# Sums of the seven half-size products moved from GpSimd to VectorE, and the tokens added by accumulating DMAs

## The chip, the cores and the metric

One core of one Trainium2 chip. The time is the device time of one execution in microseconds (us), the median of three runs; a profiled execution of the same program gives the trace. Engines are called TensorE (PE), VectorE (DVE), ScalarE (ACT), GpSimd (POOL) and SyncE (SP, which only issues DMAs here).

## The reference

An attention with mixing between heads, and behind it a token mixer and a channel mixer, all float32. The change lies in the channel mixer alone:

```python
u = x + h.transpose(0, 2, 1)                   # x, u: batch 4, 448 tokens, 768 features
h2 = np.maximum(u @ w_ch1, 0.0) @ w_ch2        # w_ch1: 768 x 1536, w_ch2: 1536 x 768
return (u + h2).astype(np.float32)
```

## The kernel before

Features lie on the partitions, tokens along the free axis. The 4 x 448 = 1792 tokens of `u` are in a DRAM tensor `u_dr` of 128 x 6 x 1792 (six tiles of 128 features).

**Split operands.** Every operand of the mixers is split into a high half (a cast to fp32r on ScalarE) and a low half (the float32 value less the high half, a subtraction on VectorE or GpSimd). One product is then three matmuls, lines 653 to 655: high x high, high x low of the second operand, low x high. The names are `wh`, `wl` for the first operand (weights), `uh`, `ul` or `rh`, `rl` for the second (tokens).

**First half of the channel mixer** (lines 889 to 921): tokens 0 to 511 (g = 0), then 512 to 767 (g = 1), in 12 chunks c of 128 hidden features. `ch1` computes a chunk (18 matmuls into `pc`), `relu_split` makes `rh` on ScalarE and `rl` on VectorE (line 650), and `ch2` of the chunk before (18 more) adds it into six PSUM banks `po`. The order on an engine is the order in which the code calls it. Between the products stand `cv_tick` (it converts the 64-bit weights of the input to float32 tiles `wt`: two instructions on VectorE at lines 456 and 460 and a third at 466, a clamp on GpSimd at 438, an absolute value on ScalarE at 432) and `split(eng)`, which splits the weights of a coming chunk, `wh` on ScalarE (412), `wl` on `eng` (413). Split number 2c belongs to `ch1` of chunk c, 2c + 1 to `ch2`.

**The stages** (lines 926 to 933): the last 1024 tokens, from SB0 = 768, go through both layers by a scheme of seven half-size products instead of eight (2 x 2 blocks, `ORDER`). For the first layer there are two groups g of seven products, for the second seven products in two halves h: 28 stages of 27 matmuls of 128 x 128 by 128 x 512. `us` holds the tokens, `rr` the hidden values. For stage n + 2 `prep_s` computes sums of quarters in place (`sum_`, line 809, on GpSimd; `w` 128 x 1152 for products 5, 6, 3 and 7, `x` 128 x 1536 for 5, 6, 7 and 4), then the high halves (835, ScalarE) and the low halves (836, VectorE), in slot n % 3 of `wslot` and `xslot`. So three stages' operands exist at a time, and those of n + 2 may be written as soon as stage n - 1 has been multiplied. `mm_s(n)` multiplies into three banks, `psx` or `psz`; the two sets are used in turn and accumulate over several products. `evict(n)` reads them out: copies on ScalarE (882, 884) or additions on VectorE (886; 877 in the second layer), `relus` on ScalarE (864). In the second layer `us` itself is the accumulator: it still holds the tokens, each product is added to it, and `store_out` writes a finished quarter to the output through SP's queue (756). As the sums of the first layer destroy one quarter of the tokens in `us`, it is loaded again from `u_dr` at stage 13 (line 933).

Of the kernel before, what the change touches and what calls it, by code (L numbers as in the profile page):

```python
# [14 lines left out]
ALU = mybir.AluOpType  # L15
# [24 lines left out]
def attn_mixer_kernel(  # L40
# [12 lines left out]
    nc = tc.nc  # L53
# [6 lines left out]
    u_dr = dram.tile([128, KD, B * S], F32, name="u_dr")  # L60
# [224 lines left out]
    p = pair("w", "pw")  # L285
# [116 lines left out]
    SP, split_at = {}, [0]  # L402

    def split(eng):
        n = split_at[0]
        split_at[0] += 1
        c, w = divmod(n % (2 * NC), 2)
        while cv_pos[0] <= min(4 * c + 2 * w + 5, len(units) - 1):
            cv_tick(1)
        src = WT[w, c // 3][:, c % 3, :]  # L410
        hi, lo = [y[:, :768] for y in wslot(n % 6)]
        nc.scalar.copy(out=hi, in_=src)
        eng.tensor_tensor(out=lo, in0=src, in1=f32(hi), op=ALU.subtract)  # L413
# [57 lines left out]
    def cv_tick(k, eng=nc.gpsimd):  # L471
        for _ in range(k):
            i = cv_pos[0]
            if i >= cv_lim[0]:
                return
            if i + 5 < len(units):
                cv_load(i + 5)
            cv_step(i, eng)
            if 0 <= i + 2 < len(units):
                cv_clamp(i + 2)  # L480
            if 0 <= i + 3 < len(units):
                cv_abs(i + 3)
            cv_pos[0] += 1
# [19 lines left out]
    for T in range(2, NT):  # L503
        hi = (sf[T] - 8) // 2
# [276 lines left out]
    def ch2(g, c, ds=range(KD)):  # L781
        i0, n = CB[g]
        ws = SP[2 * NC * g + 2 * c + 1]
        for d in ds:
            if c == 0:
                OP[g, d] = psb.tile([128, 512], F32, tag=f"o{d}", name=f"po{d}")
            mm3(OP[g, d][:, :n], [w[:, 128 * d:128 * d + 128] for w in ws], RL[g, c], c == 0, c == NC - 1)
            if c == NC - 1:
                o = UR[g][:, d, :n]
                nc.vector.tensor_tensor(out=o, in0=OP.pop((g, d))[:, :n], in1=o, op=ALU.add)  # L790
                o_row[0] = d
                store_out(i0, o)
# [12 lines left out]
        t, d = (us, 3 * j) if L == 0 else (rr, 6 * j + 3 * s)  # L805
        return t[:, d:d + 3, HN * k:HN * k + HN]

    def sum_(out, in0, in1, op=ALU.subtract):
        nc.gpsimd.tensor_tensor(out=out, in0=in0, in1=in1, op=op)  # L809

    def prep_s(n):
        L, g, p, h = stages[n]
        whi, wlo = [y.rearrange("p (a n) -> p a n", a=3) for y in wslot(n % 3)]
        xhi, xlo = [y[:, :3 * HN].rearrange("p (a n) -> p a n", a=3) for y in xslot(n % 3)]
        s = g if L == 0 else h
        A = {(i, j): a_q(L, i, j, s) for i in range(2) for j in range(2)}
        Bq = {(j, k): b_q(L, j, k, h) for j in range(2) for k in range(2)}
        tmp = rr[:, 6 + 3 * g:9 + 3 * g, :HN] if L == 0 and p in (7, 4) else None
        w, x = {1: (A[0, 0], Bq[0, 0]), 2: (A[0, 1], Bq[1, 0]), 3: (A[0, 0], Bq[1, 1]), 4: (A[1, 1], tmp or Bq[1, 0]),
                5: (A[1, 0], Bq[0, 1]), 6: (A[1, 0], Bq[0, 1]), 7: (A[1, 0], tmp or Bq[0, 0])}[p]  # L820
        if p == 5:
            sum_(w, A[1, 0], A[1, 1], ALU.add)
            sum_(x, *((Bq[0, 1], Bq[0, 0]) if L or g == 0 else (Bq[1, 1], Bq[0, 1])))
        elif p == 6:
            sum_(w, A[1, 0], A[0, 0])
            sum_(x, Bq[1, 1], Bq[0, 1])
        elif p == 3:
            sum_(w, A[0, 1], A[1, 0])
        elif p == 7:
            sum_(w, A[1, 1], A[1, 0])  # L830
            sum_(x, Bq[0, 1], Bq[0, 0])
        elif p == 4:
            sum_(x, Bq[1, 0], Bq[0, 1])
        for hi, lo, src in ((whi, wlo, w), (xhi, xlo, x)):
            nc.scalar.copy(out=hi, in_=src)  # L835
            nc.vector.tensor_tensor(out=lo, in0=src, in1=f32(hi), op=ALU.subtract)  # L836
        SW[n], SX[n] = (whi, wlo), (xhi, xlo)

    PB = {}

# [18 lines left out]
    RELU = []  # L859
# [6 lines left out]
    def evict(n):  # L866
        L, g, p, h = stages[n]
        role = "z" if p in (5, 3, 2) else "x"
        i, j = {1: (0, 0), 2: (0, 0), 5: (1, 1), 7: (1, 1), 6: (0, 1), 3: (0, 1), 4: (1, 0)}[p]
        if L == 1 and h == 0:  # L870
            return
        for m in range(3):
            ps_ = PB[role][m][:, :HN]
            d = (6 * i + 3 * g if L == 0 else 3 * i) + m
            o = (rr if L == 0 else us)[:, d, HN * j:HN * j + HN]
            if L == 1:
                nc.vector.tensor_tensor(out=o, in0=ps_, in1=o, op=ALU.add)
                if p in (2, 7, 3, 4):
                    o_row[0] = d
                    store_out(SB0 + HN * j, o)  # L880
            elif p in (1, 5, 6):
                nc.scalar.copy(out=o, in_=ps_)
            elif p == 4:
                nc.scalar.activation(out=o, in_=ps_, func=ACTF.Relu)
            else:
                nc.vector.tensor_tensor(out=o, in0=ps_, in1=o, op=ALU.add)  # L886
                RELU.append(o)

    for g in range(2):
        for c in range(NC):  # L890
            ch1(g, c)
            cv_tick(3)
            if g == 0 and c == NC - 3:
                cv_tick(1000)
                close("cv", "a1")
                usp = en("us", bufs=1, side="right")
                urp = en("urp", bufs=1)
                us = usp.tile([128, KD, 2 * HN], F32, name="us")
                load_u(0)
                load_u(1)  # L900
                nc.sync.dma_start(out=us, in_=u_dr[:, :, SB0:])
            if c and (g == 0 or c < NC - 1):
                ch2(g, c - 1)
            while split_at[0] < min(2 * (NC * g + c) + 6, 4 * NC):
                split(nc.gpsimd if g == 0 and split_at[0] % 2 else nc.vector)
            if g and c == NC - 2:
                prep_s(0)
        if g == 0:
            n = CB[1][1]
            U[1] = [y[:, :KD * n] for y in xslot(2)]  # L910
            hi, lo = [y.rearrange("p (d n) -> p d n", d=KD) for y in U[1]]
            nc.scalar.copy(out=hi, in_=UR[1])
            nc.vector.tensor_tensor(out=lo, in0=UR[1], in1=f32(hi), op=ALU.subtract)
            ch2(g, NC - 1)
        else:
            prep_s(1)
            ch2(g, NC - 2, (0, 1))
            for d in range(KD):
                ch2(g, NC - 1, (d,))
                if d + 2 < KD:  # L920
                    ch2(g, NC - 2, (d + 2,))
    close("psb", "urp", "ob", "wx")
    rp = en("rr", bufs=1)
    rr = rp.tile([128, NC, 2 * HN], F32, name="rr")
    pss = en("pss", bufs=1, space=PSUM)
    for n in range(len(stages)):
        relus()
        if n + 2 < len(stages):
            prep_s(n + 2)
        mm_s(n)  # L930
        evict(n)
        if n == 13:
            nc.sync.dma_start(out=us[:, :3, HN:], in_=u_dr[:, :3, SB0 + HN:])
    close("pss", "rr", "us", "wb", "wr", "ub", "wa")


# [36 lines left out]
```

## Time and profile before

| | |
|---|---|
| median of 3 runs | 743.91 us (742.12 to 745.8) |
| profiled execution | 742.89 us, span 741.1 us, mean granted clock 0.988 |
| TensorE busy | 709.5 us, 96% of the span |
| VectorE busy | 596.1 us, 80% |
| ScalarE busy | 392.9 us, 53% |
| GpSimd busy | 446.4 us, 60% |
| chain that ended last | PE 67%, DVE 18%, issue 7%, ACT 3%, POOL 3% |
| DMA | 105.47 MB, mean 142 GB/s |

The span runs from the first to the last instruction; 1.8 us of the profiled execution lie around it. The share of a matmul's busy time is an upper bound, since matmuls overlap: what counts is the step from the start of one to the start of the next. The chain is followed back from the last instruction, at each step to what released it.

### The profile page before, as it was taken

Reading aid. Unit: us, or ns where it says so; the run is one execution under the profiler, and the core shown is the slowest. Engines: PE = TensorE matmul, PEld = TensorE weight load, DVE = VectorE, ACT = ScalarE, POOL = GpSimd, SP = SyncE. Lnnn points to the kernel's source line nnn. Section 1 sums busy time; section 2 is a strip of 40 time slices with the busy share of each in tenths; the row PEclk is TensorE's granted clock in tenths of the full one; section 3 lists DMA queues with packets and bytes.
Section 4 is the critical chain, followed back from the end, with each engine's and each line's share of the span. In section 5 each row is a group of like instructions: output and inputs, shape, how many; then the busy total and the mean of one; then the engine's idle time right before and its main releaser. Section 6 shows DMA issues by size and latency. Waiting matters only on the chain.

```text
span 741.1 us, 19026 instructions
## 1 busy us (share of the span) xinstructions
PE 709.5 (96%) x7688; PEld 491.0 (66%) x7688; DVE 596.1 (80%) x832; ACT 392.9 (53%) x751; POOL 446.4 (60%) x291
## 2 busy tenths in 40 slices
PE   8999999999999999999999999999999979897997
PEld 4244454445445344699997888899987757685786
DVE  4777777787767879797888999865789789899992
ACT  3676666666676575464424444444554554634240
POOL 3555656665656678665657999611297297299330
PEclk9999999999999999999999999999999999999999
DMA  6788688577757644746764556750010001000022
GB/s 181 244 233 222 216 223 228 178 225 225 217 187 237 204 145 156 268 147 205 253 201 140 149 149 171 239 188 2 1 42 1 1 0 43 0 1 0 11 75 86
DMA packets 72023, 105.47 MB, mean 142 GB/s; under 512 B 23123, under 2 KB 59520, under 8 KB 71936
## 3 DMA queue, kind: packets, MB, share of 16 engines
q1 hardware_dynamic: 71360, 103.35, 45.0%
q8 instruction: 61, 1.00, 0.5%
q10 hardware_dynamic: 480, 0.87, 0.5%
q14 instruction: 26, 0.21, 0.1%
q0 software_dynamic: 96, 0.03, 0.0%
HBM read 49.18 MB, written 16.52 MB: 89 GB/s over the span
## 4 chain that ended last, share of the span: by engine, by line
PE 67%; DVE 18%; issue 7%; ACT 3%; POOL 3%; DMA 1%; SPq 0%; DVEq 0%; POOLq 0%; ACTq 0%
PE pre L174 9%; PE qk L152 9%; PE av L243 9%; PE post L214 9%; DVE ul L836 6%; DVE wl L836 4%; PE pc L655 3%; PE pc L654 3%; PE pc L653 3%; PE po L654 3%; PE po L653 3%; PE po L655 3%; DVE at L228 2%; PE pt L653 2%; PE pt L655 2%
## 5 line engine op out<-in xcount | busy, mean ns | idle before, releaser
L205 POOL TENSOR_TENSOR e<-e,sm 128x896 f32<-128x896 f32 x90 | 149.5, 1679 | 76.7 <-DVE sm L203 52.8
L158 ACT COPY s<-qk 120x896 f32<-120x896 f32 (+1 forms) x90 | 80.8, 905 | 88.0 <-PE qk L152 77.0
L191 ACT ACTIVATE e<-pre,sm 128x448 f32<-128x448 f32 x180 | 111.8, 636 | 13.9 <-DVE sm L182 9.0
L228 DVE STREAM_TRANSPOSE at<-post 128x896 f32<-128x896 f32 (+1 forms) x98 | 99.4, 1025 | 18.4 <-PE post L214 18.3
L182 DVE TENSOR_REDUCE sm<-pre 128x2 f32<-128x896 f32 x90 | 94.7, 1076 | 8.3 <-PE pre L174 8.3
L152 PE MATMUL qk<-k,q 64*64 64x448 f32 (+2 forms) x768 | 88.8, 541 | 3.6 <-DVE sm L200 2.4
L174 PE MATMUL pre<-r,kpre 64*64 64x448 f32 (+1 forms) x720 | 89.7, 553 | 2.0 <-ACT e L191 1.4
L438 POOL TENSOR_SCALAR cv_g<-cv_g 128x384 f32<-128x384 f32 (+1 forms) x52 | 82.5, 1602 | 10.5 <-ACT cv_g L432 10.4
L243 PEld LDWEIGHTS av<-at,v 64*64 64x64 f32 x2688 | 71.2, 132 | 21.0 <-ACT s L158 11.6
L836 DVE TENSOR_TENSOR wl<-wt,wh 128x1152 fp32r<-128x1152 f32 x28 | 67.0, 2393 | 18.5 <-ACT wh L835 18.5
L214 PE MATMUL post<-e,kpost 64*32 64x448 f32 x1440 | 81.2, 551 | 0.5 <-DVE at L228 0.2
L243 PE MATMUL av<-at,v 64*64 64x120 f32 (+1 forms) x2688 | 76.1, 258 | 0.6 <-ACT s L158 0.4
L654 PE MATMUL psx<-ul,wh 128*128 128x512 f32 x144 | 58.1, 403 | 6.5 <-DVE ul L836 6.5
L174 PEld LDWEIGHTS pre<-r,kpre 64*64 64x64 f32 (+1 forms) x720 | 23.7, 132 | 58.7 <-ACT e L191 30.1
L653 PE MATMUL psx<-uh,wh 128*128 128x512 f32 x144 | 57.6, 400 | 4.9 <-DVE rr L886 3.4
L152 PEld LDWEIGHTS qk<-k,q 64*64 64x64 f32 (+2 forms) x768 | 27.2, 128 | 51.0 <-DVE sm L200 25.2
L809 POOL TENSOR_TENSOR wt<-wt,wt 128x1152 f32<-128x1152 f32 x10 | 40.2, 4028 | 30.0 <-DVE wl L836 30.0
L835 ACT CAST wh<-wt 128x1152 fp32r<-128x1152 f32 x28 | 32.4, 1155 | 47.8 <-POOL wt L809 15.6
L655 PE MATMUL psx<-uh,wl 128*128 128x512 f32 x144 | 57.5, 400 | 0.0
L251 POOL COPY x<-y 128x240 f32<-128x240 f32 (+1 forms) x48 | 28.5, 598 | 41.3 <-DVE y L250 35.4
L432 ACT ACTIVATE cv_g<-cv_r 128x384 f32<-128x384 f32 (+1 forms) x52 | 28.4, 546 | 42.7 <-DVE wt L460 35.3
L655 PE MATMUL pc<-uh,wl 128*128 128x512 f32 (+1 forms) x144 | 49.3, 342 | 1.8 <-DVE wl L413 1.8
(112 smaller groups left out, 1608.4 us busy)
## 6 DMA issues: line engine op xcount, KB each, us to landing
r<-s SPq DMA_DIRECT2D x172, 210.0 KB
cv_r<-in_w_ch_dram SPq DMA_DIRECT2D x48, 384.0 KB
xr<-x_dr SPq DMA_DIRECT2D x8, 672.0 KB
u_dr<-u SPq DMA_DIRECT2D x24, 224.0 KB
k<-in_k_dram SPq DMA_DIRECT2D x20, 224.0 KB
x_dr<-x SPq DMA_DIRECT2D x36, 120.0 KB
q<-in_q_dram SPq DMA_DIRECT2D x22, 180.0 KB
v<-in_v_dram SPq DMA_DIRECT2D x16, 192.0 KB
```

Of the source, the lines that this page charges most:

```text
L152: nc.tensor.matmul(out=p[c:c + m, s, :S], lhsT=Q[T][r, h, c:c + m], rhs=K[b][r, h, :], start=True, stop=True)
L174: nc.tensor.matmul(out=p[64 * s:64 * s + 64, x, :S], lhsT=kpre[k], rhs=rt[a % NR][k], start=True, stop=True)
L182: nc.vector.tensor_reduce(out=s[:m, 0:2], in_=PP[st[0]][:m, :, :S], axis=AX.X, op=ALU.max, negate=True)
L191: nc.scalar.activation(out=E[st[0]][:m, x, :], in_=p[:m, x, :S], func=ACTF.Exp, bias=s[:m, x:x + 1], scale=1.0, accum_out=s[:m, 2 + 2 * x: ...
L205: nc.gpsimd.tensor_tensor(out=e[:m], in0=e[:m], in1=w.to_broadcast([m, 2, S]), op=ALU.mult)
L214: nc.tensor.matmul(out=p[32 * a:32 * a + 32, s, :S].rearrange("p (x g r) -> p x g r", x=2, r=32), lhsT=kpost[k, 32 * hf:32 * hf + 32], rhs ...
L228: nc.vector.transpose(out=AT[T][:, c:c + s1 - s0, :], in_=p[:, s0:s1, :S],)
L243: nc.tensor.matmul(out=p[64 * s:64 * s + 64, u, :10 * w], lhsT=V[b][k, h, j // 2 + JT * (j % 2), :], rhs=at_[k, :w, :, 32 * j + 5 * h:32 * ...
L653: nc.tensor.matmul(out=p, lhsT=a[0], rhs=x[0], start=first, stop=False, skip_group_check=on)
L654: nc.tensor.matmul(out=p, lhsT=a[0], rhs=x[1], start=False, stop=False, skip_group_check=on)
L655: nc.tensor.matmul(out=p, lhsT=a[1], rhs=x[0], start=False, stop=last, skip_group_check=on)
L836: nc.vector.tensor_tensor(out=lo, in0=src, in1=f32(hi), op=ALU.subtract)
```

## The change

The sums move from GpSimd to VectorE and are split into `sum_w` and `sum_x`, the halves into `split_s`, which now casts both operands before VectorE subtracts. The operands of the stages 0 to 2 are made at appointed chunks of the first half (`AHEAD`) and between its last products. In the loop over the chunks one split stands in front of the conversions, on VectorE, and the third `cv_tick` behind the other splits. In the second layer three quarters of the result no longer start from the tokens: the first product of each (1, 5, 6) is copied out of PSUM by ScalarE, the second (2, 7, 3) added by VectorE, and a DMA issued by GpSimd then adds the quarter into `u_dr` in DRAM, where the tokens are; from there it is stored to the output, DRAM to DRAM. The fourth quarter (product 4) is added to the tokens on VectorE as before. The reload at stage 13 is gone.

```diff
-    def sum_(out, in0, in1, op=ALU.subtract):
-        nc.gpsimd.tensor_tensor(out=out, in0=in0, in1=in1, op=op)
...
+    def sum_w(n):
+        A, _, w, _ = sources(n)
+        p = stages[n][2]
+        if p in (5, 6, 3, 7):
+            a, b = {5: (A[1, 0], A[1, 1]), 6: (A[1, 0], A[0, 0]), 3: (A[0, 1], A[1, 0]), 7: (A[1, 1], A[1, 0])}[p]
+            nc.vector.tensor_tensor(out=w, in0=a, in1=b, op=ALU.add if p == 5 else ALU.subtract)
...
+    def split_s(n, what="wx"):
...
+        for hi, lo, src in parts:
             nc.scalar.copy(out=hi, in_=src)
+        for hi, lo, src in parts:
             nc.vector.tensor_tensor(out=lo, in0=src, in1=f32(hi), op=ALU.subtract)
...
-            if L == 1:
+            if L == 1 and p == 4:
                 nc.vector.tensor_tensor(out=o, in0=ps_, in1=o, op=ALU.add)
-                if p in (2, 7, 3, 4):
-                    o_row[0] = d
-                    store_out(SB0 + HN * j, o)
+                o_row[0] = d
+                store_out(SB0 + HN * j, o)
             elif p in (1, 5, 6):
                 nc.scalar.copy(out=o, in_=ps_)
...
                 nc.vector.tensor_tensor(out=o, in0=ps_, in1=o, op=ALU.add)
-                RELU.append(o)
-
+                if L == 0:
+                    RELU.append(o)
+                else:
+                    u = u_dr[:, d, SB0 + HN * j:SB0 + HN * j + HN]
+                    nc.gpsimd.dma_start(out=u, in_=o, accum_op=ALU.add)
+                    o_row[0] = d
+                    store_out(SB0 + HN * j, u)
+
+    AHEAD = {5: [(split_s, 0, "x")], 6: [(sum_x, 1)], 7: [(sum_w, 1)], 8: [(split_s, 1, "x")], 9: [(split_s, 0, "w")],
+             10: [(split_s, 1, "w")]}
     for g in range(2):
         for c in range(NC):
             ch1(g, c)
-            cv_tick(3)
+            if split_at[0] < 2 * (NC * g + c) + 5 and split_at[0] < 4 * NC:
+                split(nc.vector)
+            cv_tick(2)
...
+            cv_tick(1)
+            if g:
+                for f, *a in AHEAD.get(c, ()):
+                    f(*a)
...
     for n in range(len(stages)):
         relus()
-        if n + 2 < len(stages):
-            prep_s(n + 2)
+        if 2 < n + 2 < len(stages):
+            sum_w(n + 2)
+            sum_x(n + 2)
+            split_s(n + 2)
         mm_s(n)
         evict(n)
-        if n == 13:
-            nc.sync.dma_start(out=us[:, :3, HN:], in_=u_dr[:, :3, SB0 + HN:])
```

How instructions move, at three places. First VectorE where the second layer begins: the last eviction of product 2 of the first layer (`psz`), then what is made for stages 15 and 16. Before:

```order
L886 TENSOR_TENSOR rr<-psz_7654,rr 128x512
L836 TENSOR_TENSOR wl<-wt_5618,wh 128x1152
L836 TENSOR_TENSOR ul<-rr,uh 128x1536
L836 TENSOR_TENSOR wl<-wt_4778,wh 128x1152
L836 TENSOR_TENSOR ul<-rr,uh 128x1536
```

Now:

```order
L891 TENSOR_TENSOR rr<-psz_7654,rr 128x512
L843 TENSOR_TENSOR wl<-wt_5618,wh 128x1152
L843 TENSOR_TENSOR ul<-rr,uh 128x1536
L823 TENSOR_TENSOR wt_4778<-wt_4778,wt_5620 128x3x384
L831 TENSOR_TENSOR rr<-rr 128x3x512
L843 TENSOR_TENSOR wl<-wt_4778,wh 128x1152
L843 TENSOR_TENSOR ul<-rr,uh 128x1536
```

The sums of stage 16 (lines 823 and 831) stand on VectorE between the low halves of stages 15 and 16; they were rows of line 809 on GpSimd.

Second VectorE at chunk 0 of the first half, from `rl` of this chunk to `rl` of the next. Before:

```order
L650 SCALAR_TENSOR_TENSOR rl<-pc_5632,rh 128x512
L456 TENSOR_SCALAR cv_g<-cv_g 128x384
L460 SCALAR_TENSOR_TENSOR wt_5618<-cv_r,cv_g 128x384
L466 SCALAR_TENSOR_TENSOR wt_5618<-cv_r,wt_5618 128x384
L456 TENSOR_SCALAR cv_g<-cv_g 128x384
L460 SCALAR_TENSOR_TENSOR wt_5618<-cv_r,cv_g 128x384
L466 SCALAR_TENSOR_TENSOR wt_5618<-cv_r,wt_5618 128x384
L456 TENSOR_SCALAR cv_g<-cv_g 128x384
L460 SCALAR_TENSOR_TENSOR wt_4779<-cv_r,cv_g 128x384
L466 SCALAR_TENSOR_TENSOR wt_4779<-cv_r,wt_4779 128x384
L413 TENSOR_TENSOR wl<-wt_4777,wh 128x768
L650 SCALAR_TENSOR_TENSOR rl<-pc_5691,rh 128x512
```

Now:

```order
L650 SCALAR_TENSOR_TENSOR rl<-pc_5632,rh 128x512
L413 TENSOR_TENSOR wl<-wt_4778,wh 128x768
L456 TENSOR_SCALAR cv_g<-cv_g 128x384
L460 SCALAR_TENSOR_TENSOR wt_5618<-cv_r,cv_g 128x384
L466 SCALAR_TENSOR_TENSOR wt_5618<-cv_r,wt_5618 128x384
L456 TENSOR_SCALAR cv_g<-cv_g 128x384
L460 SCALAR_TENSOR_TENSOR wt_5618<-cv_r,cv_g 128x384
L466 SCALAR_TENSOR_TENSOR wt_5618<-cv_r,wt_5618 128x384
L413 TENSOR_TENSOR wl<-wt_4777,wh 128x768
L456 TENSOR_SCALAR cv_g<-cv_g 128x384
L460 SCALAR_TENSOR_TENSOR wt_4779<-cv_r,cv_g 128x384
L466 SCALAR_TENSOR_TENSOR wt_4779<-cv_r,wt_4779 128x384
```

Split 4 (`wt_4777`, for `ch1` of chunk 2) stood behind nine conversion instructions and stands behind six; split 3 (`wt_4778`), which was GpSimd's, is in front of them. From chunk 1 on the even split is in front of all nine.

Third SP's queue at the end, with the semaphores that each DMA waits for (DMASW: a DMA of GpSimd's; DMAHW: one of SP's own). Now:

```order
L756 DMA out_dram<-u_dr 128x384 [waits DMAHW4_49]
L756 DMA out_dram<-u_dr 128x128 [waits DMAHW5_49,DMASW3_49]
L756 DMA out_dram<-u_dr 128x384 [waits DMAHW6_49]
L756 DMA out_dram<-us 128x128 [waits DMAHW7_49,DVE_49]
L756 DMA out_dram<-us 128x384 [waits DMAHW0_49]
L756 DMA out_dram<-us 128x128 [waits DMAHW1_49,DVE_49]
```

The rows with `u_dr` were `out_dram<-us` and waited for VectorE; the last of product 2's now waits for an accumulating DMA, and product 4's stores stand behind it.

## Rows read from the trace of the kernel before

**Rows 1.** Busy time by stretch, TensorE to GpSimd, then clock and DMA

```profile
484.00:540.00 56.00, 55.81 (x447) 54.64 (x447) 39.45 (x43) 26.94 (x38) 9.84 (x4) 1.00 0.13 46
540.00:737.00 197.00, 180.53 (x762) 144.84 (x760) 168.24 (x97) 88.06 (x94) 120.41 (x30) 0.97 0.07 22
```

**Rows 2.** Timeline of TensorE: start, duration, line, operation, tiles

```profile
540.46 0.40 PE L653 MATMUL psx<-uh,wh 128*128 128x512 f32 x1
...
572.89 0.39 PE L653 MATMUL psz<-uh,wh 128*128 128x512 f32 x1
...
578.78 0.39 PE L655 MATMUL psz<-uh,wl 128*128 128x512 f32 x1
...
736.60 0.39 PE L655 MATMUL psx<-uh,wl 128*128 128x512 f32 x1
```

**Rows 3.** Waits of TensorE, 540 to 742 us: total, times, longest

```profile
PE psx L654 <- DVE ul L836: 6.5, 4, 2.8
PE psz L654 <- DVE ul L836: 5.1, 4, 2.3
PE psx L653 <- DVE rr L886: 3.4, 3, 2.8
PE psx L653 <- ACT rr L882: 1.4, 1, 1.4
```

**Rows 4.** Busy time by stretch again: two in which the clock fell

```profile
400.00:407.00 7.00, 6.07 (x20) 4.87 (x21) 6.79 (x12) 3.01 (x5) 6.27 (x5) 0.76 0.44 134
600.00:607.00 7.00, 4.03 (x10) 2.98 (x11) 7.00 (x2) 6.10 (x9) 6.92 (x3) 0.76 0.00 0
```

**Rows 5.** Timeline of VectorE and GpSimd in the stages

```profile
554.45 4.62 POOL L809 TENSOR_TENSOR rr<-us 128x1536 f32<-128x1536 f32 x1
555.62 5.05 DVE L836 TENSOR_TENSOR ul<-us,uh 128x1536 fp32r<-128x1536 f32 x1
...
582.31 1.36 DVE L836 TENSOR_TENSOR wl<-wt,wh 128x1152 fp32r<-128x1152 f32 x1 [1.74 <-ACT wh L835]
583.69 1.76 DVE L836 TENSOR_TENSOR ul<-us,uh 128x1536 fp32r<-128x1536 f32 x1
```

**Rows 6.** Groups by line and shape, 540 to 742 us: busy, mean, idle before

```profile
L836 DVE TENSOR_TENSOR wl<-wt,wh 128x1152 fp32r<-128x1152 f32 x26 | 64.3, 2472 | 17.2 <-ACT wh L835 17.2
L836 DVE TENSOR_TENSOR ul<-rr,uh 128x1536 fp32r<-128x1536 f32 x18 | 49.6, 2756 | 0.0
...
L836 DVE TENSOR_TENSOR ul<-us,uh 128x1536 fp32r<-128x1536 f32 x9 | 33.1, 3676 | 0.7 <-ACT uh L835 0.7
L835 ACT CAST wh<-wt 128x1152 fp32r<-128x1152 f32 x26 | 30.1, 1156 | 47.8 <-POOL wt L809 15.6 <-PE psx L654 11.0 <-PE psz L654 8.1
L835 ACT CAST uh<-rr 128x1536 fp32r<-128x1536 f32 x18 | 26.6, 1477 | 13.0 <-POOL rr L809 13.0
```

**Rows 7.** Timeline of VectorE and TensorE, first chunks of the channel mixer

```profile
391.26 0.69 DVE L650 SCALAR_TENSOR_TENSOR rl<-pc,rh 128x512 fp32r<-128x512 f32 x1 [3.06 <-ACT rh L649]
398.31 2.57 DVE L413 TENSOR_TENSOR wl<-wt,wh 128x768 fp32r<-128x768 f32 x1
398.75 0.39 PE L654 MATMUL pc<-ul,wh 128*128 128x512 f32 x1
400.93 0.50 PE L655 MATMUL pc<-uh,wl 128*128 128x512 f32 x1 [1.79 <-DVE wl L413]
406.12 0.95 DVE L413 TENSOR_TENSOR wl<-wt,wh 128x768 fp32r<-128x768 f32 x1
```

**Rows 8.** Timeline of VectorE, last instruction

```profile
737.03 0.69 DVE L877 TENSOR_TENSOR us<-psx,us 128x512 f32<-128x512 f32 x1 [1.35 <-PE psx L655]
```

**Rows 9.** DMAs issued by GpSimd: count, KB each, us from issue to landing

```profile
kcat<-in_wcat_dram POOLq DMA_DIRECT2D x2, 8.0 KB, 3.9
```

**Rows 10.** Busy time of two chunks, and the clamps' group on the page

```profile
407.00:423.00 16.00, 16.00 (x72) 13.28 (x71) 15.17 (x23) 6.91 (x13) 15.08 (x9) 1.00 0.55 152
...
L438 POOL TENSOR_SCALAR cv_g<-cv_g 128x384 f32<-128x384 f32 (+1 forms) x52 | 82.5, 1602 | 10.5 <-ACT cv_g L432 10.4
```

More of the change, by code (lines that the diff above doesn't have):

```diff
@@ L806, in b_q, with sources @@
         return t[:, d:d + 3, HN * k:HN * k + HN]
-    def sum_(out, in0, in1, op=ALU.subtract):
-        nc.gpsimd.tensor_tensor(out=out, in0=in0, in1=in1, op=op)
-    def prep_s(n):
+    def sources(n):
         L, g, p, h = stages[n]
-        whi, wlo = [y.rearrange("p (a n) -> p a n", a=3) for y in wslot(n % 3)]
-        xhi, xlo = [y[:, :3 * HN].rearrange("p (a n) -> p a n", a=3) for y in xslot(n % 3)]
         s = g if L == 0 else h
@@ L820, in prep_s, with sum_x @@
                 5: (A[1, 0], Bq[0, 1]), 6: (A[1, 0], Bq[0, 1]), 7: (A[1, 0], tmp or Bq[0, 0])}[p]
[L821 to L834, printed above, removed]
+        return A, Bq, w, x
+    def sum_w(n):
[4 more added lines that the diff above has]
+            nc.vector.tensor_tensor(out=w, in0=a, in1=b, op=ALU.add if p == 5 else ALU.subtract)
+    def sum_x(n):
+        _, Bq, _, x = sources(n)
+        L, g, p, h = stages[n]
+        if p in (5, 6, 7, 4):
+            a, b = {5: (Bq[0, 1], Bq[0, 0]) if L or g == 0 else (Bq[1, 1], Bq[0, 1]), 6: (Bq[1, 1], Bq[0, 1]),
+                    7: (Bq[0, 1], Bq[0, 0]), 4: (Bq[1, 0], Bq[0, 1])}[p]
+            nc.vector.tensor_tensor(out=x, in0=a, in1=b, op=ALU.subtract)
+    def split_s(n, what="wx"):
+        t = {"w": (SW, wslot, 384), "x": (SX, xslot, HN)}
+        parts = []
+        for y in what:
+            to, slot, m = t[y]
+            to[n] = [z[:, :3 * m].rearrange("p (a n) -> p a n", a=3) for z in slot(n % 3)]
+            parts.append((*to[n], sources(n)["wx".index(y) + 2]))
+        for hi, lo, src in parts:
             nc.scalar.copy(out=hi, in_=src)
+        for hi, lo, src in parts:
             nc.vector.tensor_tensor(out=lo, in0=src, in1=f32(hi), op=ALU.subtract)
-        SW[n], SX[n] = (whi, wlo), (xhi, xlo)
     PB = {}
@@ L905, in attn_mixer_kernel @@
                 split(nc.gpsimd if g == 0 and split_at[0] % 2 else nc.vector)
-            if g and c == NC - 2:
-                prep_s(0)
+            cv_tick(1)
+            if g:
+                for f, *a in AHEAD.get(c, ()):
+                    f(*a)
         if g == 0:
@@ L921, in attn_mixer_kernel @@
                     ch2(g, NC - 2, (d + 2,))
+                if d < 2:
+                    (sum_w, sum_x)[d](2)
+            split_s(2)
     close("psb", "urp", "ob", "wx")
```

1 line of the change is left out of this document (removed).

## The prediction

> **What bounds the kernel now.** The change touches two places: the 28 stages of half-size products at the end, and the first half of the channel mixer. I first read the busy time of the stretch that holds the stages [rows 1]: TensorE is not full there, VectorE is busy for 168.24 of 197 us, GpSimd for 120.41. Then the times of single matmuls [rows 2]. One stage is 27 matmuls; in an undisturbed one the first starts at 572.89 and the last at 578.78, which is 26 steps in 5.89 us, so 0.2265 us for a matmul and 6.12 us for a stage. The first matmul of the 28 stages starts at 540.46, the last at 736.60. These are 755 steps in 196.1 us; at 0.2265 us they would take 171.0. **So 25.1 us are lost between the stages.**
>
> Whose they are is in TensorE's waits [rows 3]: 6.5 + 5.1 us on the low half of a second operand (line 836), 3.4 + 1.4 us on a PSUM bank that is not yet read out, 16.4 us in 12 waits. Three stretches follow in which the granted clock is down; one reads 0.76 over 7 us [rows 4], so 0.24 x 7 = 1.7 us of clock each, 5.0 in all. Each came right behind a long wait. Of the rest (3.7 us), 2.0 are in the way a wait is counted: it begins at the end of the matmul before, 0.39 us after its start, where the next was due after 0.2265, so 0.16 us are missing in each of the 12.
>
> Why VectorE is late is in the rows of single instructions [rows 5]. The low half of a second operand takes 1.76 us when GpSimd is idle (583.69) and 5.05 when it stands beside a GpSimd sum (555.62, with the sum of 554.45). First operand: 1.36 us alone. Over the stages the means are 64.3/26 = 2.47 us and (49.6 + 33.1)/27 = 3.06 us [rows 6]. The GpSimd sums thus cost twice: 4.62 us each in the chain sum, ScalarE cast, VectorE difference, and up to three times the price for VectorE's own instructions beside them.
>
> The Trainium skill (SBUF — State Buffer, Who interferes with whom) says that a VectorE instruction with two SBUF inputs and a GpSimd one that reads SBUF never share: the later is blocked until the first is done. The rows agree roughly: 5.05 us is a 1.76 us instruction with some 3.3 us of a 4.6 us sum in front. It would make VectorE's own price 1.36 and 1.76 once GpSimd is empty, which the rows at 582 us show without it.
>
> **The change, part by part.**
>
> *Sums on VectorE.* Of 16 sums for first operands and 16 for second ones, those of stages 1 and 2 (two of each) are made ahead, so 14 pairs fall into the stages. VectorE has no row for such a sum; it is the same kind of instruction as the low half (two float32 inputs of the same size in SBUF), so I take 1.36 + 1.76 = 3.12 us for a pair; the other end is the mean beside GpSimd, 2.47 + 3.06 = 5.53. I take 3.12 because GpSimd has no sum left to run beside it. VectorE's work over the stages is then 26 pairs of low halves (81.1 us), 14 pairs of sums (43.7) and evictions. These were 13 groups of three and become 10 (products 1, 5 and 6 of the second layer go to ScalarE): 30 x 0.69 [rows 8] = 20.7. In all 145.5 us, 85% of TensorE's 171.0. It is not the bound.
>
> Nor is a single stage: what stage n + 2 needs may be written when stage n starts (three slots in turn) and is due 12.2 us later. The worst list is an eviction (2.1), two sums (3.1), two low halves (3.1), and even with both casts in series (1.16 + 1.48 [rows 6]) it is 10.9 us. The eviction of stage n stands behind that list, and its bank is wanted only at the start of stage n + 2, so the 3.4 us of waits on banks go as well. ScalarE has two casts, 2.6 us, and three evictions or Relus in the 6.12. **I take back 24.6 of the 25.1 us**, and leave 0.5 for a late hand-over here and there.
>
> *Operands made ahead.* Two low-half pairs move by some 10 us, and three sums come into chunks where VectorE is less loaded (39 of 56 us busy between 484 and 540 [rows 1]); nothing on TensorE waits for them until the stages. Cost nothing, and if that cover were gone, at most their 4 us.
>
> *Splits earlier in the first half.* TensorE lost one wait there [rows 7]: a matmul at 398.75 is followed only at 400.93, 1.95 us late, because the low half that chunk 2 wants stood at 398.31 behind nine conversion instructions and took 2.57 us beside GpSimd (0.95 at 406.12). The clock fell behind it as well [rows 4], 1.7 us more: 3.6 in all. Now one split stands in front of the conversions and this one behind six of them: rl ends at 391.95, and the nine conversions took the 6.4 us to 398.31, so six about 4.2. With the split in front and the split itself, 0.95 to 2.57 us each, it is ready at 398.1 to 401.3, against a need at 398.98: between nothing lost and 2.3 us. GpSimd has a split less beside them, so I take the early end but for a remnant, a **gain of 3.0**; the other end is 0.
>
> *Accumulating DMAs.* Product 2's second half is evicted two stages before the end, so the last three are issued some 12.2 - 2.1 = 10.1 us before TensorE's last matmul ends. DMAs issued by GpSimd, small ones, landed after 3.9 us at the median [rows 9]. At that the copies to the output can start 6.2 us before the end, and the first store of product 4, behind them on SP's queue, is due 3.4 us before it. So I take **0**; the last store's 3.4 us from 737.72 to the span's end stay. Other end: three that land one after another (11.7 us) would put the copies 1.6 us behind the last matmul, and the stores behind those: +4. By the Trainium skill (DMA: Bandwidth & Descriptors, Anatomy of one DMA) 2.0 us plus 256 KB at 436 GB/s are 2.6 us, which changes nothing here. The removed reload of three tiles kept no engine waiting.
>
> **The sum:** 742.9 (the profiled execution) - 24.6 - 3.0 + 0 = 715.3. The median of the three runs is 1.0 us above that execution, so I forecast **716.0**. Its own range is 713 to 718.5. A measurement of this kernel tells about 0.5%, 3.7 us, from no change.
>
> **The rivals.**
>
> A. *The end comes late.* The accumulating DMAs are slower than any row here, and SP holds the last six stores behind the copies that wait for them. For it: they read and write DRAM, which no row prices. Against it: 6 us of slack. 1 to 5 us more: about 719. Chance 0.10.
>
> B. *VectorE becomes the bound in the first half of the channel mixer.* It is busy 15.17 of 16 us there [rows 10], 7.6 of the 8.15 us (36 x 0.2265) of a chunk. The split now stands where GpSimd runs its clamps of 1.6 us [rows 10]. Were it held for a whole clamp, a chunk needs 9.2 us and TensorE waits 1.0 in each of some ten: 742.9 - 24.6 + 10.5 = 729. Against it: the conversions meet the same clamps already, and the 15.17 include that. The Trainium skill's rule on the shared port (SBUF — State Buffer, Who interferes with whom), taken to the clamps, would have it so. Chance 0.06.
>
> C. *VectorE stays as slow as now and becomes the bound: slower.* If the long low halves had another cause than GpSimd's sums, 40 pairs at 5.53 us and 20.7 of evictions are 242 us where the stages take 196 now: 742.9 - 3.0 + 46 = 786. It decides from (196.1 - 20.7)/40 = 4.4 us a pair. Then the change doesn't do what it says. Against it: alone, the rows read 1.36 and 1.76. Chance 0.04.
>
> **How the numbers follow.** Forecast 0.78, A 0.10, B 0.06, C 0.04, the rest (0.02) between forecast and no change. Faster by over 0.5%: forecast, A, B and half the rest, 0.95; within 0.5%: 0.01; slower: C, 0.04. The range is 713 to 722: below, all 28.7 us back and a run 1 us under the profiled one; above, rival A. B, C and some of the forecast's edge are left out, 0.15.
>
> **What would show it.** Right: TensorE steps of 0.2265 us through all stages, 171 to 172 us from first to last; no low half over 1.8 us in the stages; sums near 1.36 and 1.76 us; clock at 1.00 from 407 us on; no wait at 398 us. A shows as a last store more than 3.4 us behind the last eviction, with SP waiting on POOL's DMAs. B shows as waits on L413 or L650 between 386 and 484 us. Wrong altogether: VectorE full through the stages with long low halves and no GpSimd work beside them.

## The result, and the profile after

| | before | after |
|---|---|---|
| median | 744.72 us (4 runs, 742.12 to 745.8) | 719.12 us (4 runs, 718.02 to 722.37) |
| profiled execution | 742.89 us, span 741.1, clock 0.988 | 718.02 us, span 716.2, clock 1.000 |
| channel mixer, first half: first matmul to the first of the stages | 386.27 to 540.46: 154.19 us | 384.56 to 540.51: 155.95 us |
| stages: first to last matmul | 540.46 to 736.60: 196.14 us | 540.51 to 711.67: 171.16 us |
| last matmul to the end of the span | 4.51 us | 4.57 us |

After/before is 0.9668 (95%: 0.9627 to 0.971). The profiled executions differ by 24.87 us: the stages give 24.98, the first half takes 1.76, the attention ahead of it, which the change doesn't touch, came out 1.71 shorter, and the end took 0.06.

Busy time by stretch of the kernel after (columns as in [rows 1]: TensorE, its weight loads, VectorE, ScalarE, GpSimd, then clock and DMA); the last line answers to the second of [rows 1], the one above it to the first:

```profile
386.00:407.00 21.00, 21.00 (x94) 17.40 (x93) 17.49 (x25) 9.66 (x16) 13.37 (x8) 1.00 0.46 129
407.00:437.00 30.00, 30.00 (x134) 24.83 (x133) 29.17 (x44) 12.75 (x21) 25.72 (x16) 1.00 0.58 160
437.00:484.00 47.00, 42.77 (x185) 34.09 (x184) 41.19 (x61) 20.17 (x33) 34.19 (x20) 1.00 0.66 208
484.00:540.00 56.00, 55.81 (x447) 54.64 (x446) 40.46 (x49) 27.96 (x39) 1.86 (x1) 1.00 0.12 42
540.00:712.00 172.00, 172.00 (x762) 142.22 (x760) 141.54 (x114) 93.68 (x103) 8.04 (x9) 1.00 0.16 34
```

TensorE is full through the stages, GpSimd has gone from 120.41 us to the 8.04 of nine DMA issues, and the clock, 0.97 on average in [rows 1], reads 1.00. The stretch that is now not full is 437 to 484, in the first half. The two ends of the stages, TensorE's timeline as in [rows 2]:

```profile
540.51 0.40 PE L653 MATMUL psx<-uh,wh 128*128 128x512 f32 x1
...
711.67 0.39 PE L655 MATMUL psx<-uh,wl 128*128 128x512 f32 x1
```

755 steps in 171.16 us are 0.2267 us each: the step of an undisturbed stage. The waits of [rows 3] have no successor: TensorE has none after 540. All that it has from 386 us on is one group:

```profile
PE po L654 <- DVE rl L650: 4.2, 4, 1.2
```

VectorE's groups by shape, 540 to 717 us (busy, mean ns of one, idle before), to be read against [rows 6]; line 843 was 836, lines 823 and 831 are the sums:

```profile
L843 DVE TENSOR_TENSOR wl<-wt,wh 128x1152 fp32r<-128x1152 f32 x26 | 35.2, 1354 | 15.3 <-ACT wh L841 15.1
L843 DVE TENSOR_TENSOR ul<-rr,uh 128x1536 fp32r<-128x1536 f32 x18 | 31.6, 1758 | 3.7 <-ACT uh L841 3.4
...
L831 DVE TENSOR_TENSOR rr<-rr 128x1536 f32<-128x1536 f32 x8 | 14.0, 1750 | 0.0
L823 DVE TENSOR_TENSOR wt<-wt,wt 128x1152 f32<-128x1152 f32 x9 | 12.2, 1351 | 0.0
```

The low halves went from 2472 and 2756 ns to 1354 and 1758, the prices that the two undisturbed rows of [rows 5] had shown. A sum costs VectorE 1.35 and 1.75 us. The end, first by the DMA view (count, KB each, us from issue to landing):

```profile
u_dr<-us POOLq DMA_DIRECT2D x9, 256.0 KB, 5.9
```

And by the timelines of SP's queue and of VectorE:

```profile
682.53 25.93 SPq L756 DMA_DIRECT2D out_dram<-u_dr  x18
708.73 4.88 SPq L756 DMA_DIRECT2D out_dram<-us  x6
...
712.09 0.69 DVE L883 TENSOR_TENSOR us<-psx,us 128x512 f32<-128x512 f32 x1 [1.35 <-PE psx L655]
```

The accumulating DMAs land after 5.9 us at the median, not 3.9, but the copies behind them leave the queue before the last stores are due: from the last eviction's end (712.78) to the end of the span are 3.4 us, as before.

### The profile page after: what moved, and what is told of

It is laid out like the page before. It is cut to its first block, busy times and chain, and to the rows that moved or that the text cites. A ratio compares the mean times of both kernels' runs of the same rounds, so it can differ in the third digit from the quotient of the medians.

```text
span 716.2 us, 19005 instructions
## 1 busy us (share of the span) xinstructions
PE 698.9 (98%) x7688; PEld 487.3 (68%) x7688; DVE 572.7 (80%) x856; ACT 400.3 (56%) x760; POOL 320.6 (45%) x267
## 4 chain that ended last, share of the span: by engine, by line
PE 76%; DVE 15%; issue 4%; DMA 2%; ACT 1%; POOL 1%; SPq 0%; DVEq 0%; POOLq 0%; ACTq 0%
PE pre L174 9%; PE qk L152 9%; PE av L243 9%; PE post L214 9%; PE psx L655 5%; PE psx L654 5%; PE psx L653 5%; DVE cv_g L456 4%; PE psz L655 3%; PE psz L654 3%; PE psz L653 3%; DVE wt L460 3%; DVE at L228 2%; PE pt L653 2%; PE pt L654 2%
## 5 line engine op out<-in xcount | busy, mean ns | idle before, releaser
L896 POOL DMA_DIRECT2D u_dr<-us x9 | 8.0, 1128 | 207.4 <-DVE us L891 207.4
L438 POOL TENSOR_SCALAR cv_g<-cv_g 128x384 f32<-128x384 f32 (+1 forms) x52 | 79.6, 1547 | 11.0 <-ACT cv_g L432 10.9
L152 PEld LDWEIGHTS qk<-k,q 64*64 64x64 f32 (+2 forms) x768 | 27.5, 127 | 50.2 <-DVE sm L200 24.6
L653 PE MATMUL psx<-uh,wh 128*128 128x512 f32 x144 | 56.0, 389 | 0.0
L654 PE MATMUL psx<-ul,wh 128*128 128x512 f32 x144 | 56.0, 389 | 0.0
L655 PE MATMUL psx<-uh,wl 128*128 128x512 f32 x144 | 56.0, 389 | 0.0
L654 PE MATMUL po<-rl,wh 128*128 128x512 f32 (+1 forms) x144 | 49.0, 340 | 4.3 <-DVE rl L650 4.2
L843 DVE TENSOR_TENSOR wl<-wt,wh 128x1152 fp32r<-128x1152 f32 x28 | 37.9, 1354 | 17.3 <-ACT wh L841 17.0
L412 ACT CAST wh<-wt 128x768 fp32r<-128x768 f32 x48 | 39.6, 831 | 19.4 <-PE po L654 11.0
```

The source lines that it names most:

```text
L152: nc.tensor.matmul(out=p[c:c + m, s, :S], lhsT=Q[T][r, h, c:c + m], rhs=K[b][r, h, :], start=True, stop=True)
L653: nc.tensor.matmul(out=p, lhsT=a[0], rhs=x[0], start=first, stop=False, skip_group_check=on)
L654: nc.tensor.matmul(out=p, lhsT=a[0], rhs=x[1], start=False, stop=False, skip_group_check=on)
L655: nc.tensor.matmul(out=p, lhsT=a[1], rhs=x[0], start=False, stop=last, skip_group_check=on)
```

## Where the first half lost it

In the first half VectorE converts the weights, and what a chunk costs it depends on whether three or four conversions fall into it. One chunk of four (chunk 6), kernel after, timelines of VectorE and GpSimd (start, duration, line; brackets: idle before and its releaser):

```profile
441.90 0.68 DVE L650 SCALAR_TENSOR_TENSOR rl<-pc,rh 128x512 fp32r<-128x512 f32 x1
442.50 0.35 DVE L456 TENSOR_SCALAR cv_g<-cv_g 128x384 uint32<-128x384 uint32 x1
442.88 0.56 DVE L460 SCALAR_TENSOR_TENSOR wt<-cv_r,cv_g 128x384 uint32<-128x384 uint32 x1
...
447.96 2.13 POOL L413 TENSOR_TENSOR wl<-wt,wh 128x768 fp32r<-128x768 f32 x1 [1.44 <-ACT wh L412]
448.31 2.00 DVE L456 TENSOR_SCALAR cv_g<-cv_g 128x384 uint32<-128x384 uint32 x1
450.35 0.74 DVE L460 SCALAR_TENSOR_TENSOR wt<-cv_r,cv_g 128x384 uint32<-128x384 uint32 x1
...
451.60 0.68 DVE L650 SCALAR_TENSOR_TENSOR rl<-pc,rh 128x512 fp32r<-128x512 f32 x1
```

From one `rl` to the next are 9.70 us, where TensorE needs 36 x 0.2267 = 8.16 for the chunk. 1.65 of them are one instruction: L456 takes 0.35 us, but 2.00 at 448.31, where it starts just behind GpSimd's split (447.96) and ends just after it (450.09). Five chunks run so (4 to 8). `rl`'s head start, from its end to the matmul that reads it, shrinks by the difference: 2.41 us at chunk 4, 0.87 at chunk 5, 0.06 at chunks 6 to 9, and those are the four waits. TensorE's timeline at the second of them:

```profile
450.71 0.39 PE L653 MATMUL po<-rh,wh 128*128 128x512 f32 x1
452.33 0.50 PE L654 MATMUL po<-rl,wh 128*128 128x512 f32 x1 [1.24 <-DVE rl L650]
```

A step of 1.63 us in place of 0.23. In the kernel before the chunks of four were 5 to 8. At 9.37 us they too took longer than TensorE's 8.16; VectorE's `rl` of two neighbours:

```profile
441.44 0.68 DVE L650 SCALAR_TENSOR_TENSOR rl<-pc,rh 128x512 fp32r<-128x512 f32 x1
...
450.81 0.68 DVE L650 SCALAR_TENSOR_TENSOR rl<-pc,rh 128x512 fp32r<-128x512 f32 x1
```

There the head start at chunk 4 was 6.80 us, and fell to 1.58 by chunk 9. TensorE had been held at 398 and had run on a lower clock behind it [rows 4, 7], and each delay of TensorE is head start for VectorE. The run with the sums alone (below) shows it on unchanged code.

## The experiments

**The changed kernel once more**, on one chip with the next three.

> The changed kernel once more beside the others, for their differences: stretch 156.0, stages 171.2, run 718 to 722 us.

Median 719.4 us (four runs), ratio 0.9674 (0.9644 to 0.9704). The profiled execution has the stages at 171.16 and the first half at 155.98: both lengths repeat to 0.03 us. (The stages also read 171.16 in each of the next three runs and in the one with the fourth quarter through DRAM.) The attention took 386.81 us, against 384.56 the first time: what moves from run to run is ahead of the change.

**The chunks as before, all else as after:**

```diff
-            if split_at[0] < 2 * (NC * g + c) + 5 and split_at[0] < 4 * NC:
-                split(nc.vector)
-            cv_tick(2)
+            cv_tick(3)
...
-            cv_tick(1)
```

> The changed kernel with the loop over the chunks in the order of the kernel before (three conversions, no split in front). From the first matmul of the channel mixer to the first of the stages it took 154.2 us before and 156.0 in the changed kernel: one wait of 2.0 us with a fall of the clock (1.6) went, four waits on rl of 5.2 us in all came. Both theories: the stretch is 154.2 again, with the wait near 398 us and without the four; the stages stay at 171.2. 1.8 us below the changed kernel's run.

The first half takes 154.08 us, what it took before (154.19), and the stages keep 171.16. So the earlier splits cost 1.9 us beside this run instead of bringing 3.0. That the total is the one of before is in part chance: the wait near 400 is there (a step of 2.16 us), but the clock did not fall behind it, and two more waits came instead (steps of 0.72 and 0.94 at 467 and 476). Median 719.27, ratio 0.9674 (0.9647 to 0.9702): the 1.9 us of the trace is not resolved by the times. The waits are those of a split that comes late, and none is on `rl`; TensorE's, 386 to 540 us:

```profile
PE pc L655 <- DVE wl L413: 2.7, 3, 1.8
```

**The early split at chunk 0 alone**, the other chunks in their old order:

```diff
-            if split_at[0] < 2 * (NC * g + c) + 5 and split_at[0] < 4 * NC:
+            if g == c == 0:
                 split(nc.vector)
-            cv_tick(2)
+            cv_tick(3 if g or c else 2)
...
-            cv_tick(1)
+            if g == c == 0:
+                cv_tick(1)
```

> The early split in chunk 0 alone, the other chunks ordered as in the kernel before. Theory 1 (VectorE is the bound in the chunks with four conversions, 9.4 to 9.7 us against TensorE's 8.15, and lives on the head start of rl, which the wait near 398 us used to lengthen by 3.6 us): no wait near 398 us, head start about 2 us at chunk 1, used up at chunk 8, 1 to 2 us of waits on rl at chunks 8 and 9; stretch 151.5 to 152.5. Theory 2 (the moved split alone is to blame, as it draws conversions forward): no wait at all, stretch 150.6.

153.86 us: above both. The wait at 398 is gone, and four others came, on L413, with steps of 0.47 to 1.31 us at 416 to 477 (2.8 us over four usual steps). So the splits moved in the later chunks are not the only source of waits: those were in their old place here. Take one wait away, and TensorE comes early to the next thing that VectorE has not finished. Where exactly it then waits was not foreseen: I had `rl` in mind, and it was the split. Median 718.43, ratio 0.9664 (0.9626 to 0.9703).

**No split on GpSimd in the loop:**

```diff
-                split(nc.gpsimd if g == 0 and split_at[0] % 2 else nc.vector)
+                split(nc.vector)
```

> The changed kernel with every split of the chunk loop on VectorE; GpSimd keeps the clamps. Theory 1 with its second half (in each chunk one VectorE instruction of 0.35 or 0.56 us stands blocked behind GpSimd's split and takes 2.0 to 2.2, so that split costs VectorE 1.65 us where doing it itself costs 0.95): a chunk with four conversions takes 9.0 us instead of 9.7, those before it gain head start, waits on rl 0 to 1 us, stretch 150.6 to 151.6, 4 to 5 us below the changed kernel. Theory 2: four waits stay, VectorE has one split more, stretch 156 or more.

The first half takes 150.12 us, TensorE waits for nothing from 386 us to the end of the stages, and the median is 713.72 (0.961, 0.9575 to 0.9645): **this beats both kernels**, the changed one by 5.7 us (719.4 on the same chip). Its busy time in two stretches that hold the loop, to be read against the first three lines of after:

```profile
386.00:437.00 51.00, 51.00 (x226) 42.24 (x225) 46.14 (x78) 24.65 (x40) 33.58 (x20) 1.00 0.58 161
437.00:480.00 43.00, 43.00 (x191) 35.63 (x190) 37.27 (x63) 18.58 (x29) 23.59 (x13) 1.00 0.71 230
```

TensorE is full in both. VectorE has more to do and is done sooner: a chunk of four with two splits of its own takes it 8.96 us instead of 9.70. The split that it took over costs 0.95 us (445.36 below); left to GpSimd it had cost 1.65. VectorE is still slower than TensorE in these chunks, and its head start falls from 5.02 us at chunk 4 to 1.03 at chunk 9: it just lasts. The clamps stayed on GpSimd, and beside them VectorE's rows lengthen by no more than 0.31 us (L456, 0.35 to 0.66). GpSimd's and VectorE's timelines:

```profile
443.89 3.77 POOL L438 TENSOR_SCALAR cv_g<-cv_g 128x384 f32<-128x384 f32 x2 [0.50 <-ACT cv_g L432]
...
444.11 0.74 DVE L460 SCALAR_TENSOR_TENSOR wt<-cv_r,cv_g 128x384 uint32<-128x384 uint32 x1
444.89 0.56 DVE L466 SCALAR_TENSOR_TENSOR wt<-cv_r,wt 128x384 uint32<-128x384 uint32 x1
445.36 0.95 DVE L413 TENSOR_TENSOR wl<-wt,wh 128x768 fp32r<-128x768 f32 x1
446.23 0.66 DVE L456 TENSOR_SCALAR cv_g<-cv_g 128x384 uint32<-128x384 uint32 x1
```

**The sums back on GpSimd, all else as after** (`nc.vector` to `nc.gpsimd` in `sum_w` and `sum_x`):

> The changed kernel with all sums on GpSimd again; operands made ahead, casts before low halves, copies on ScalarE and accumulating DMAs stay. Theory 1 (the sums' place is the whole gain): stages 190 to 196 us instead of 171.2, waits on low halves and banks as before, low halves up to 5 us beside the sums. Rival (the order of casts and the evictions on ScalarE carry much of it): 171 to 184 us.

745.25 us (one run), stages 194.19. TensorE's waits, 540 to 742 us, are those of [rows 3] again:

```profile
PE psx L654 <- DVE ul L843: 6.8, 4, 2.8
PE psz L654 <- DVE ul L843: 4.6, 2, 2.3
PE psx L653 <- DVE rr L891: 2.7, 1, 2.7
PE psx L653 <- ACT rr L887: 0.9, 1, 0.9
```

VectorE's group of the first operand's low halves is back at a mean of 2.40 us:

```profile
L843 DVE TENSOR_TENSOR wl<-wt,wh 128x1152 fp32r<-128x1152 f32 x26 | 62.4, 2398 | 19.5 <-ACT wh L841 19.5
```

The stages are 1.95 us shorter than before: that is all the other parts are worth while the sums stand on GpSimd.

**The other way round: the kernel before, with nothing but its sums on VectorE:**

```diff
-        nc.gpsimd.tensor_tensor(out=out, in0=in0, in1=in1, op=op)
+        nc.vector.tensor_tensor(out=out, in0=in0, in1=in1, op=op)
```

> The kernel before with one word changed: the sums of the seven products on VectorE instead of GpSimd, in the old order (first operand's sum, second's, cast, low half, cast, low half); no splits moved, no accumulating DMAs, the reload at stage 13 and all operands of stage 0 and 1 as before. Theory (the sums' place alone is the gain): the stages take 171.2 to 173 us from first to last matmul, where before has 196.1; the stretch from the first matmul of the channel mixer's first half to the first of the stages keeps the 154.2 us of before, with its wait at about 398; the execution 717 to 721 us. Rival (it takes the new order of casts and low halves, the operands made ahead and the lighter evictions as well): waits on low halves of line 836 or on banks stay, and the stages take 176 us or more.

Stages 175.57 us, between the two (the rival had asked for 176); execution 722.56 (one run), beside 742.41 for before. One word of the code brings 20.6 of the 25.0 us; of the 4.4 that are left, 3.8 are the steps of three waits, TensorE's from 540 on:

```profile
PE psx L653 <- DVE ur L790: 1.5, 1, 1.5
PE psx L654 <- DVE ul L836: 1.3, 1, 1.3
PE psz L654 <- DVE ul L836: 0.6, 1, 0.6
```

The first is in neither kernel. Behind the last chunk VectorE now makes the sums and low halves of stage 1 (536.96 to 543.28) before it reads out the six banks of `po`, one of which stage 0 wants. VectorE's timeline:

```profile
541.52 1.76 DVE L836 TENSOR_TENSOR ul<-us,uh 128x1536 fp32r<-128x1536 f32 x1 [0.28 <-ACT uh L835]
543.20 2.07 DVE L790 TENSOR_TENSOR ur<-po,ur 128x256 f32<-128x256 f32 x6
```

The first half of this run bears on the head start. Up to its last chunk the code is that of the kernel before. The wait near 399 is there too (a step of 2.18 us), but behind it the granted clock stayed at 1.00, so that TensorE kept the 1.6 us that the clock had cost it before. `rl`'s head start at chunk 9 was then 0.46 us instead of 1.58, and two waits came that the kernel before did not have (steps of 0.54 and 0.93 at 466.66 and 475.28). The first half took 153.83 us, only 0.36 less. TensorE's waits, 386 to 540 us:

```profile
PE pc L655 <- DVE wl L413: 2.5, 3, 1.8
```

**Nothing ahead:** the changed kernel, with the operands of stages 0 and 1 made at the places of before and those of stage 2 in the loop:

```diff
-    AHEAD = {5: [(split_s, 0, "x")], 6: [(sum_x, 1)], 7: [(sum_w, 1)], 8: [(split_s, 1, "x")], 9: [(split_s, 0, "w")],
-             10: [(split_s, 1, "w")]}
+    AHEAD = {10: [(sum_w, 0), (sum_x, 0), (split_s, 0)]}
...
+            sum_w(1)
+            sum_x(1)
+            split_s(1)
             ch2(g, NC - 2, (0, 1))
...
-                if d < 2:
-                    (sum_w, sum_x)[d](2)
-            split_s(2)
...
-        if 2 < n + 2 < len(stages):
+        if n + 2 < len(stages):
```

> The changed kernel, but the operands of the stages 0 and 1 are made at the places of the kernel before (stage 0 at chunk 10, stage 1 behind the chunks), and those of stage 2 in the loop over the stages. My step (the operands made ahead cost nothing and bring nothing): stages 171.2 us from first to last matmul, the stretch of the first half 156.0 as with the change. Rival (making them ahead is what keeps the first stages free of waits): waits on low halves of line 843 in the stages 0 to 3, the stages take 172 to 176 us, or the first half ends 1 to 4 us later.

First half 155.97, stages 172.91 us (execution 721.66, one run). The time lies where the rival had it, the place does not. Making them ahead costs nothing, as I said, but it does bring something, 1.75 us: it is the first of the three waits of the sums alone, on the eviction of `po`, a step of 1.84 us at 543.55, not a wait on a low half. TensorE's timeline:

```profile
543.55 0.39 PE L655 MATMUL psx<-uh,wl 128*128 128x512 f32 x1
545.39 0.50 PE L653 MATMUL psx<-uh,wh 128*128 128x512 f32 x1 [1.45 <-DVE ur L790]
```

**The tokens as before:** every product of the second layer added to `us` on VectorE, no accumulating DMA, the reload at stage 13 back.

```diff
-            if L == 1 and p == 4:
+            if L == 1:
                 nc.vector.tensor_tensor(out=o, in0=ps_, in1=o, op=ALU.add)
-                o_row[0] = d
-                store_out(SB0 + HN * j, o)
+                if p in (2, 7, 3, 4):
+                    o_row[0] = d
+                    store_out(SB0 + HN * j, o)
...
+        if n == 13:
+            nc.sync.dma_start(out=us[:, :3, HN:], in_=u_dr[:, :3, SB0 + HN:])
```

> The changed kernel with the tokens added as before: us accumulates on VectorE from the tokens, the quarter is loaded again at stage 13, stores from us, no accumulating DMA. VectorE has three groups of evictions more, 6.2 us. Theory 1 (neither way of adding is on the path): stages 171.2 to 171.7, last matmul to the end 4.5 us, run 718 to 720. Rival (the copies on ScalarE were needed to keep VectorE below TensorE): 2 to 6 us of new waits in the stages.

Stages 172.55 us, 1.39 more, most of it in one wait of 0.9 on a low half (a step of 1.27 us at 677.94); execution 722.11 (one run). It is above the first range and below the rival's. The accumulating DMAs free VectorE of three evictions in each of three stages, and that is worth 1.4 us; no wait on the DMAs themselves shows, and the end takes 4.57 us with them and 4.51 without.

The sums alone had a wait at the same low half. VectorE's row for it there (L836) and here (L843):

```profile
677.83 1.76 DVE L836 TENSOR_TENSOR ul<-rr,uh 128x1536 fp32r<-128x1536 f32 x1 [0.36 <-ACT uh L835]
...
677.40 1.76 DVE L843 TENSOR_TENSOR ul<-rr,uh 128x1536 fp32r<-128x1536 f32 x1 [0.36 <-ACT uh L841]
```

Counted from the first matmul of the stages (540.67 and 543.27) it starts at 137.16 and at 134.13 us. From the low halves of stage 2 on, both runs have the same instructions in the same order on VectorE and on ScalarE, VectorE's always some 3.0 us apart, and the stages differ by 3.02. What differs is the work that VectorE still has to do when the stages begin. So while VectorE has all these evictions, the operands made ahead are worth 3.0 us, not 1.75; and the casts that `split_s` calls before the low halves change no engine's order.

**The fourth quarter through DRAM as well** (product 4's evictions become copies, followed by accumulating DMAs and the copies to the output):

```diff
-                nc.vector.tensor_tensor(out=o, in0=ps_, in1=o, op=ALU.add)
+                nc.vector.tensor_copy(out=o, in_=ps_)
+                u = u_dr[:, d, SB0 + HN * j:SB0 + HN * j + HN]
+                nc.gpsimd.dma_start(out=u, in_=o, accum_op=ALU.add)
                 o_row[0] = d
-                store_out(SB0 + HN * j, o)
+                store_out(SB0 + HN * j, u)
```

> The changed kernel with product 4's quarter added by accumulating DMAs too. In the changed kernel the nine land after 5.9 us at the median and are hidden, as the last are issued 12 us before the end. Theory 1 (they are slow, and hidden only by their place): from the last matmul to the end 11 to 14 us instead of 4.6, run 6 to 9 us longer. Rival (an accumulating DMA costs about what a store costs): 5 to 8 us.

From the last matmul to the end are 10.8 us instead of 4.6, just under the first range; execution 725.55 (one run). Timelines of GpSimd and of SP's queue:

```profile
714.34 0.86 POOL L885 DMA_DIRECT2D u_dr<-us  x1 [1.18 <-DVE us L883]
...
704.76 15.69 SPq L756 DMA_DIRECT2D out_dram<-u_dr  x12
```

So the delay that rival A feared exists: where an accumulating DMA and a copy stand behind the last product, the end comes 6.2 us later. The change leaves product 4 out of this, and its end takes 4.57 us.

**Is it GpSimd's presence, or the chain through its sums?** The changed kernel with 12 subtractions on GpSimd in the second layer, 128 x 1152, whose results nobody reads:

```diff
+        if n >= 16:
+            z = WT[0, 0]
+            nc.gpsimd.tensor_tensor(out=z[:, :, :384], in0=f32(SW[n][0]), in1=z[:, :, 384:], op=ALU.subtract)
```

> The changed kernel with 12 subtractions of 128 x 1152 on GpSimd, one for each of stages 16 to 27, from the high half of the first operand into a tile that nobody reads any more; nothing waits for their result. Theory 1 with contention (GpSimd's reading blocks VectorE's two-operand instructions): low halves and sums beside them take 3 to 4 us, VectorE's 86 us for these stages become 100 or more, stages 179 to 191 us. Rival (GpSimd's sums cost only by standing in the chain): 171.2 us as in the changed kernel, low halves 1.36 and 1.76.

Stages 193.73 us, above my range (179 to 191) and far from the rival's 171.2; execution 743.37 (one run), where before was 745.8. Work that nobody waits for takes back 22.6 of the 25 us. TensorE's waits from 540 on:

```profile
PE psx L654 <- DVE ul L843: 10.6, 5, 4.5
PE psz L654 <- DVE ul L843: 3.3, 2, 1.7
```

GpSimd's timeline beside VectorE's:

```profile
632.12 2.94 POOL L846 TENSOR_TENSOR wt<-wh,wt 128x1152 f32<-128x1152 f32 x1 [143.93 <-ACT wh L841]
...
632.43 3.84 DVE L843 TENSOR_TENSOR wl<-wt,wh 128x1152 fp32r<-128x1152 f32 x1
```

The low half of 632.43 ends 1.21 us after GpSimd's subtraction (635.06), as if it had stood still until that was over and then run about its usual 1.35. That is the Trainium skill's rule (SBUF — State Buffer, Who interferes with whom): a VectorE instruction with two SBUF inputs and a GpSimd one that reads SBUF exclude each other, and the later is blocked until the first ends. These rows agree. So blocking alone can cost nearly as much as the sums did; how the 25 us of the kernel before divide between blocking and the chain of sum, cast and low half, no run shows.

## Why the prediction was right, and where it was not

The forecast was 716.0 (713 to 722); measured 719.12. That is above the forecast's own range (713 to 718.5). It lies in the stated range because that was drawn out to rival A, which did not come, so this part is luck. (715.3 and the 1.0 us are 716.3, not 716.0.) By its own steps:

- **Sums on VectorE: right in size, not all in cause.** 24.6 of 25.1 us were to come back; 24.98 did, with no hand-over late. A pair was taken at 3.12 us and costs 3.10. But the step put all of it on the sums' place. The sums alone bring 20.6, the operands made ahead another 3.0 (sums alone against tokens as before), the lighter evictions the last 1.4 (tokens as before against after). Taken out by themselves the operands made ahead are worth only 1.75 (nothing ahead): the two parts relieve the same engine, and are not independent. "The worst list is 10.9 us" assumed a list that starts with its stage; at the seam VectorE still owed the banks of `po`, and without the lighter evictions it was late once more at 678.
- **Operands made ahead: cost nothing, as said;** the gain of 1.75 to 3.0 was not foreseen. Four sums come ahead, not three: 6.2 us, not 4.
- **Splits earlier in the first half: wrong.** The step "a gain of 3.0" looked at the one wait it removed. That went, and the fall of the clock behind it, as foreseen. But the load of 15.17 of 16 us [rows 10] (7.7 us of a chunk, not 7.6) was read between 407 and 423, where the chunks have three conversions. In those of four the same trace has 9.37 us against TensorE's 8.16: VectorE was short of time there, and had lived on the 3.6 us by which TensorE had been held back. Measured +1.76 instead of -3.0, which is nearly all that the sum missed on the stretches touched. This is rival B's place and bound in a mild form: four waits, not ten, and held by GpSimd's splits; beside the clamps, which rival B blamed, VectorE's rows lengthen by 0.2 to 0.3 us.
- **Accumulating DMAs: 0, as said,** with the term behind it mis-sized: 5.9 us to land at the median (6.5 for the last) where 3.9 was taken. The 6 us of slack took it. Rival A did not come; the run with the fourth quarter in DRAM shows what it would have been.
- **Rival C** (long low halves with another cause) fell: 1354 and 1758 ns.

The sum missed the profiled execution by 718.02 - 715.3 = 2.7 us: the first half's 4.8 too good, less 1.7 that the attention, which the change does not touch, happened to be shorter, and 0.4 of the stages. Without that accident the miss would have been 4.4.

## What to carry to other kernels

Two-input work handed to GpSimd was not free for VectorE here: a subtraction that takes VectorE 0.95 us cost it 1.65 as GpSimd's, and 12 that nobody waited for cost this kernel 22.6. Price such an edit in VectorE's own longer rows, and try the work on VectorE first. And before a removed wait is booked as a gain, compare the follower's time per period with TensorE's: where it is longer, the wait was its head start, and can come back further on.

## What the runs showed of the hardware that was not expected

- An instruction of one SBUF input is held as well: L456 took 2.00 us for 0.35 beside GpSimd's two-input split. Beside GpSimd's one-input clamps the rows shown lengthen by no more than 0.31 us (0.35 to 0.66), and a two-input subtraction (445.36 in the run without splits on GpSimd) not at all. So the rule on the shared port, taken to the clamps as rival B took it, is not what these rows show.
- An accumulating DMA of 256 KB into DRAM lands after 5.9 us at the median (5.4 over the twelve of the fourth-quarter run). They are issued in threes, one right behind the other: the first of each three lands after 4.1 to 4.5 us, the third after 6.1 to 6.6. The Trainium skill's fit (DMA: Bandwidth & Descriptors, Anatomy of one DMA) would give an estimate of 2.6; the rows disagree, those of the first ones too.
- A like gap, another clock: behind the step of 2.18 us at 398.75 the granted clock read 0.76 over 7 us [rows 4, 7]; behind one of 2.16 at 400.04, in the run with the chunks as before, it read 1.00:

```profile
402.00:409.00 7.00, 6.80 (x30) 5.64 (x31) 6.79 (x14) 3.51 (x6) 6.27 (x4) 1.00 0.47 126
```
